# One 2 MB gradient store cut into a 120-row and an 8-row transfer, eight pairs before the end of a decoder-block backward pass

## The chip, the cores and the metric

The kernel runs on one core of a Trainium2 chip. The metric is device time in microseconds (us) for one launch, the median of several executions. The launch computes the forward pass and all gradients of one decode step of a transformer block. It uses the core's five engines: TensorE (PE in the profile, its weight loads PEld), VectorE (DVE), ScalarE (ACT), GpSimd (POOL) and SyncE (SP). Data moves between HBM and the on-chip memory through the core's 16 DMA engines. Nearly all transfers here are issued by SP, in the order in which the program writes them.

## The reference

The block takes a token for each of 4 sequences (512 values each), 32 heads of 128, and a key and a value cache of 4096 positions for each of the 4 x 32 = 128 heads:

```
q      = layernorm(x) @ wq                           # 4 x 32 heads x 128
p      = softmax(q . k_cache / sqrt(128))            # 128 heads x 4096
o      = p . v_cache
h      = x + o @ wo
out    = h + (silu(LN(h) @ w1) * (LN(h) @ w3)) @ w2
grads  = vjp(out; grad_out) for x, k_cache, v_cache, wq, wo, w1, w3, w2
```

The two large results are the gradients of the caches. For each head, dV is the outer product of p (4096) and the gradient of o (128), and dK is the outer product of dS (4096) and q (128). Each is 4096 x 128 values in bf16, 1 MB a head, so 128 MB for dK and 128 MB for dV. The caches, which must be read, are of the same size.

## The kernel before, in words

All large tiles live in one tile `arena` of 23 slots, each a little over 8 KB on each of 128 partitions (`Slot`); `Slot2` takes two neighbouring slots, for two heads at once. A slot is taken when a tile is made and given back when its last reader has been issued; the framework puts in the semaphore waits that make the reuse safe, so a slot whose content is being stored is written again only when that store has landed.

**First part** (to about 700 us). For each head, K and V are loaded (1 MB each, lines 181 and 189), scores and softmax are computed, and K and V are reduced to what the later steps need.

**Second part.** V is loaded again, transposed in place on TensorE and ScalarE (lines 805 and 806), multiplied with the gradient of o to give dP (line 1363 for pairs), and turned into dS. VectorE then writes the outer products. The first 32 heads (`SP = 32`) are done one at a time; the other 96 are done as 48 pairs (`NT`), t = 0 to 47. A pair's gradient takes two slots and is stored by one transfer of 128 rows of 8192 bf16 values, 16 KB a row: 64 rows for each of the two heads. The function that does it is `grad_pair` (line 1441). Its VectorE work is `outer_pair` (line 1434), one multiply of 128 x 8192, and its store is line 1444. It is called for dV (`out_3`) by `more_V` and for dK (`out_2`) by the loop over t. The loop, for each t: loads the V of pair t + 3 where one is left (line 1331), runs that pair's transposes and dP with a slice of the side work between them (`side`: the gradients of the weights), runs `more_V`, which keeps dV a little ahead of dK, and then stores dK of pair t:

```
grad_pair(out_2, t, pdS[t // 2][:, t % 2], reps["rq", "p", t // B][:, t % B, :])
```

SP issues all of this in one queue. After the dK store of t = 40, that queue holds 16 more transfers: a load of V (2 MB), two pair stores, the last load of V, the last 1 MB store of the side work (line 1190), and eleven pair stores.

The row view that the store uses is

```
ap[b, h:h + 2].rearrange("h (p j) d -> (h p) (j d)", p=P // 2)
```

which is 128 rows of 16 KB, one for each partition. Completion of SP's transfers is counted on eight semaphores in turn: each transfer takes the next one and is issued only when the transfer that used it eight issues before has landed.

Of the kernel before, what the change touches and what calls it, by code (L numbers as in the profile page):

```python
# [28 lines left out]
def kernel(  # L29
# [22 lines left out]
    nc = tc.nc  # L52
    P = nc.NUM_PARTITIONS
# [5 lines left out]
    Dh = A_k_cache.shape[3]  # L59
# [6 lines left out]
    SJ = Sk // P  # L66
# [144 lines left out]
    for i in range(2):  # L211
        t = fcon.tile([P, 64], BF16, name=f"onesw{i}")
# [4 lines left out]
    def ones_window(col):  # L217
# [11 lines left out]
                          in_=rowg[:, None, :, None].to_broadcast([P, 4, 8, 4]))  # L229
# [758 lines left out]
    with ExitStack() as c2:  # L988
# [325 lines left out]
        NT = (NH - SP) // 2  # L1314
# [8 lines left out]
        def two_heads(ap, t):  # L1323
            b, h = t % B, H0 + t // B * 2
            return ap[b, h:h + 2].rearrange("h (p j) d -> (h p) (j d)", p=P // 2)
# [107 lines left out]
        def outer_pair(dst, col2, row):  # L1433
            nc.vector.tensor_tensor(  # L1434
                out=dst.rearrange("p (j r t) -> p j r t", r=Dh // 2, t=2),
                in0=col2[:, :, None, :].to_broadcast([P, 2 * SJ, Dh // 2, 2]),
                in1=row.rearrange("p (r t) -> p r t", t=2)[:, None, :, :].to_broadcast([P, 2 * SJ, Dh // 2, 2]),
                op=ALU.mult,
            )

        def grad_pair(out_ap, t, col2, row):
            g_ = Slot2()
            outer_pair(g_.t[:, 0:2 * SJ * Dh], col2, row)
            nc.sync.dma_start(out=two_heads(out_ap, t), in_=g_.t[:, 0:2 * SJ * Dh])
            g_.give()

        O0, S0, S1, L, LP = 2, 21, 35, 5, 3
# [2 lines left out]
        def more_V(upto):  # L1450
            while gvd["n"] < min(SP, upto):
                s = gvd["n"]
                P_pairs(s)
                replicate("rdo", s - s % REP)
                grad_V(s)
                P_pairs(s + 1)
                P_pairs(s + 2)
                gvd["n"] += 1
                if s % REP == 2 and s + 2 < SP:
                    replicate("rdo", s + 2)  # L1460
                elif s % REP == 2:
                    replicate_pair("rdo", 0)
                if s >= SP - 2:
                    P2_pair(s - SP + 2)
            while gvd["t"] < NT and SP + 2 * gvd["t"] + 2 <= upto:
                t = gvd["t"]
                P2_pair(t)
                replicate_pair("rdo", t // B)
                grad_pair(out_3, t, pP2.pop(t), reps["rdo", "p", t // B][:, t % B, :])
                P2_pair(t + 1)  # L1470
                gvd["t"] += 1
                if t % B == 2:
                    replicate_pair("rdo", t // B + 1)
# [59 lines left out]
        for t in range(NT):  # L1533
            s = SP + 2 * t
            load_pairs(t + LP)
            if t % B == 2:
                replicate_pair("rq", t // B + 1)
            if t + LP < NT:
                front_pair(t + LP, lambda: side(s))
            else:  # L1540
                if t + LP == NT:
                    rows_out()
                    rows_T()
                side(s)
            more_V(s + 2 + lead_V(s))
            grad_pair(out_2, t, pdS[t // 2][:, t % 2], reps["rq", "p", t // B][:, t % B, :])
            if t % 2 == 1 and t + 1 < NT:
                group_dS_pair((t + 1) // 2)
            side(s + 1)
# [31 lines left out]
```

## Time and profile before

| what | value |
|---|---|
| median of 3 runs | 1683.99 us (1683.85 to 1684.81) |
| the profiled execution, its own time | 1683.33 us |
| its span, first to last instruction | 1681.5 us |
| mean granted TensorE clock | 0.869 |
| busy share of PE, DVE, ACT, POOL | 74%, 74%, 57%, 25% |
| moved by DMA | 707.16 MB, mean 421 GB/s |
| pair stores of 2048 KB (line 1444) | 96, median 27.5 us from issue to landing |
| loads of V for a pair, 2048 KB (line 1331) | 48, median 31.7 us |
| one `outer_pair` on DVE | 4.4 us |

The page gives engine shares for the whole span, a row of 40 slices with the mean busy share of the 16 DMA engines, and the chain of work that ended last. For one stage, the table of stretches is the view to read: a line has the start and end of the stretch, its length, the busy time of each engine with its number of instructions, the granted clock, the mean busy share of the 16 DMA engines and the rate in GB/s. A share of 0.06 is one engine of the sixteen at work. In the order of instructions, "SPq" is SP issuing a transfer; the time beside it covers all that is merged into the line, waits included.

### The profile page before, as it was taken

Reading aid. Unit: us, or ns where it says so; the run is one execution under the profiler, and the core shown is the slowest. Engines: PE = TensorE matmul, PEld = TensorE weight load, DVE = VectorE, ACT = ScalarE, POOL = GpSimd, SP = SyncE. Lnnn points to the kernel's source line nnn. Section 1 sums busy time; section 2 is a strip of 40 time slices with the busy share of each in tenths; the row PEclk is TensorE's granted clock in tenths of the full one; section 3 lists DMA queues with packets and bytes.
Section 4 is the critical chain, followed back from the end, with each engine's and each line's share of the span. In section 5 each row is a group of like instructions: output and inputs, shape, how many; then the busy total and the mean of one; then the engine's idle time right before and its main releaser. Section 6 shows DMA issues by size and latency. Waiting matters only on the chain.

```text
span 1681.5 us, 33231 instructions
## 1 busy us (share of the span) xinstructions
PE 1243.9 (74%) x13784; PEld 874.1 (52%) x13784; DVE 1238.8 (74%) x1204; ACT 957.5 (57%) x1482; POOL 412.9 (25%) x732
## 2 busy tenths in 40 slices
PE   5889888888888888877777657567766776776750
PEld 4777776667666776644433335444444443444430
DVE  5989899999999987767766467576655656655682
ACT  3455454445445544677666556666665676676650
POOL 1221222222232223444552323211100011111110
PEclk9999999999999999999999878886667667676675
DMA  9999999999999999999999999999999999999996
GB/s 401 424 425 425 425 424 425 424 425 424 418 424 412 424 404 407 412 409 425 426 426 428 430 430 429 429 430 430 430 430 429 431 429 431 430 429 429 431 431 277
DMA packets 80983, 707.16 MB, mean 421 GB/s; under 512 B 8748, under 2 KB 12984, under 8 KB 15296
## 3 DMA queue, kind: packets, MB, share of 16 engines
q1 hardware_dynamic: 80416, 704.94, 99.4%
q8 instruction: 108, 1.77, 0.4%
q14 instruction: 43, 0.35, 0.0%
q0 software_dynamic: 416, 0.10, 0.0%
HBM read 422.59 MB, written 282.34 MB: 419 GB/s over the span
## 4 chain that ended last, share of the span: by engine, by line
DMA 40%; DVE 8%; PE 5%; ACT 4%; issue 3%; POOL 2%; DVEq 0%; SPq 0%; ACTq 0%; POOLq 0%
DMA out_dram<-arena 37%; DVE arena L1434 6%; ACT arena L806 3%; DMA arena<-in_A_v_cache_dram 3%; POOL zd L1246 1%; PE pt_tps L805 1%; PE M_ps L475 1%; DVE arena L460 1%; PE dq_ps L1032 1%; PE dP_ps L1280 1%; DMA arena<-arena 0%; PE pt_wo L613 0%; POOL P L1251 0%; ACT Pn L439 0%; POOL arena L1431 0%
## 5 line engine op out<-in xcount | busy, mean ns | idle before, releaser
L806 ACT COPY arena<-pt_tps 128x1024 bf16<-128x1024 bf16 x512 | 491.1, 1026 | 239.2 <-PE pt_tps L805 236.1
L805 PE MATMUL pt_tps<-ident_f,arena 128*128 128x128 f32 x2048 | 397.0, 346 | 195.4 <-DMA arena<-in_A_v_cache_dram 111.7
L805 PEld LDWEIGHTS pt_tps<-ident_f,arena 128*128 128x128 f32 x2048 | 290.8, 175 | 362.7 <-issue 187.3
L1434 DVE TENSOR_TENSOR arena<-arena 128x8192 bf16<-128x8192 bf16 x48 | 212.4, 4425 | 206.6 <-DMA out_dram<-arena 176.3
L475 PE MATMUL M_ps<-arena 128*128 128x130 bf16 x4096 | 285.9, 222 | 43.7 <-DMA arena<-in_A_v_cache_dram 43.2
L460 DVE TENSOR_TENSOR arena<-arena 128x4096 bf16<-128x4096 bf16 x128 | 292.4, 2285 | 24.3 <-POOL arena L456 24.3
L475 PEld LDWEIGHTS <-arena 128*128 128x128 bf16 x4096 | 252.3, 99 | 65.1 <-DMA arena<-in_A_v_cache_dram 58.1
L1434 DVE TENSOR_TENSOR arena<-dS,arena 128x8192 bf16<-128x8192 bf16 x48 | 212.4, 4426 | 63.6 <-DMA out_dram<-arena 63.6
L367 DVE STREAM_TRANSPOSE arena<-arena 128x512 f32<-128x512 f32 (+1 forms) x321 | 250.5, 796 | 0.0
L362 ACT COPY arena<-pt_tps 128x1024 bf16<-128x1024 bf16 x128 | 129.4, 1012 | 189.4 <-PE pt_tps L361 147.4
L373 POOL TENSOR_TENSOR W<-qrep,wmask 128x128 bf16<-128x128 bf16 x128 | 120.0, 938 | 85.6 <-PE S_ps L393 71.2
L1431 POOL COPY arena<-arena 128x128 bf16<-128x128 bf16 x48 | 45.2, 941 | 374.5 <-DVE arena L1434 248.6
L456 POOL COPY arena<-P_all 128x64 bf16<-128x64 bf16 x128 | 32.4, 253 | 413.1 <-ACT P_all L450 410.0
L1343 POOL COPY arena<-arena 64x4 bf16<-64x4 bf16 x96 | 78.5, 818 | 127.7 <-PE dP_ps L1363 118.2
L1363 PE MATMUL dP_ps<-arena 128*32 128x512 bf16 x768 | 85.3, 478 | 8.4 <-ACT arena L806 7.9
L450 ACT COPY P_all<-pt_P 32x64 bf16<-32x64 bf16 x256 | 51.9, 203 | 54.6 <-PE pt_P L446 52.4
L820 DVE TENSOR_TENSOR arena<-dS,arena 128x4096 bf16<-128x4096 bf16 x32 | 73.3, 2292 | 12.7 <-DMA out_dram<-arena 12.3
L361 PE MATMUL pt_tps<-ident_b,arena 128*128 128x128 bf16 x1024 | 80.5, 223 | 0.0
L820 DVE TENSOR_TENSOR arena<-P,arena 128x4096 bf16<-128x4096 bf16 x29 | 66.4, 2293 | 18.4 <-DMA out_dram<-arena 17.3
L485 PE MATMUL kP_ps<-arena,onesw 128*32 128x512 bf16 x1024 | 79.6, 388 | 0.0
L393 PE MATMUL S_ps<-arena,W 128*32 128x256 bf16 x1536 | 75.2, 286 | 0.5 <-DVE arena L367 0.2
L439 ACT ACTIVATE Pn<-E,rl 128x1024 bf16<-128x1024 f32 x64 | 73.7, 1151 | 3.2 <-DVE rl L436 3.2
(257 smaller groups left out, 1402.3 us busy)
## 6 DMA issues: line engine op xcount, KB each, us to landing
out_dram<-arena SPq DMA_DIRECT2D x96, 2048.0 KB, 27.5
arena<-in_A_v_cache_dram SPq DMA_DIRECT2D x160, 1024.0 KB, 15.9
arena<-in_A_k_cache_dram SPq DMA_DIRECT2D x128, 1024.0 KB, 15.5
arena<-in_A_v_cache_dram SPq DMA_DIRECT2D x48, 2048.0 KB, 31.7
out_dram<-arena SPq DMA_DIRECT2D x72, 1024.0 KB, 19.8
arena<-in_A_wq_dram SPq DMA_DIRECT2D x8, 1024.0 KB, 17.8
arena<-in_B_w_dram SPq DMA_DIRECT2D x8, 896.0 KB, 14.9
out_dram<-arena SPq DMA_DIRECT2D x6, 896.0 KB, 26.5
```

The source lines that it names most:

```text
L361: nc.tensor.transpose(pt[:, i, :], Kn[:, c * GW + i, :], ident_b[:])
L362: nc.scalar.copy(out=KT[:, c * GW:(c + 1) * GW, :], in_=pt[:])
L367: nc.vector.transpose(out=KT[:, c * w_:(c + n) * w_], in_=Kn[:, c * w_:(c + n) * w_])
L373: nc.gpsimd.tensor_tensor(out=W[:, hl], in0=qrep[:, :, s:s + 1].to_broadcast([P, 4, 32]), in1=wmask[:, hl, None, :].to_broadcast([P, 4, 32 ...
L460: nc.vector.tensor_tensor(out=PK[:, :, 0:Dh].rearrange("p j (r t) -> p j r t", t=2), in0=Ks[s].heads().rearrange("p j (r t) -> p j r t", t=2),
L475: nc.tensor.matmul(hold["M"][:], lhsT=Vn[:, j, :], rhs=PK[:, j, :], start=(j == 0), stop=(j == SJ - 1))
L485: nc.tensor.matmul(hold["kP"][32 * q:32 * (q + 1), :, :], lhsT=ones_window(w), rhs=PK[:, j0:j0 + 4, 0:Dh], start=(w == 0 and c == 0), stop ...
L805: nc.tensor.transpose(ptw[:, jj, :], w[:, 4 * g + jj, :], ident_f[:])
L806: nc.scalar.copy(out=v.rearrange("p (j d) -> p j d", d=Dh)[:, g * GW:(g + 1) * GW, :], in_=pt[:])
L820: nc.vector.tensor_tensor(out=dst.rearrange("p j (r t) -> p j r t", t=2), in0=col2[:, :, None, :].to_broadcast([P, SJ, Dh // 2, 2]), in1=r ...
L1363: nc.tensor.matmul(rows["acc"][32 * c:32 * (c + 1), :], lhsT=zt[t % B][:, k, ZP - m:ZP - m + 32], rhs=words_of(v, 2 * c + u, k), start=(pl ...
L1434: nc.vector.tensor_tensor(out=dst.rearrange("p (j r t) -> p j r t", r=Dh // 2, t=2), in0=col2[:, :, None, :].to_broadcast([P, 2 * SJ, Dh / ...
```

## The change

Inside `grad_pair`, one store out of 96 is cut in two: the dK store of the pair t = NT - 8 = 40. Partitions 0 to 119 go in a first transfer and partitions 120 to 127 in a second one right behind it. Together they carry the same 2 MB to the same addresses. All other stores are issued as one transfer as before. The slots are given back after the last of the transfers.

```diff
         def grad_pair(out_ap, t, col2, row):
             g_ = Slot2()
             outer_pair(g_.t[:, 0:2 * SJ * Dh], col2, row)
-            nc.sync.dma_start(out=two_heads(out_ap, t), in_=g_.t[:, 0:2 * SJ * Dh])
+            cuts = (0, 120, P) if out_ap is out_2 and t == NT - 8 else (0, P)
+            for p0, p1 in zip(cuts, cuts[1:]):
+                nc.sync.dma_start(out=two_heads(out_ap, t)[p0:p1], in_=g_.t[p0:p1, 0:2 * SJ * Dh])
             g_.give()
```

In the order of instructions, SP has one row more (527 instead of 526); the order on the other engines is the same. The semaphore that each later transfer takes moves on by one, and the waits with it. The next tile in the slots of the cut store waits for two semaphores instead of one.

## The prediction

> **What bounds the kernel now.** I read the page's slices first, then the stretches at the end, then the DMA view of a stretch, SP's and DVE's order around the cut store, and the chain of waits. The page:
>
> ```profile
> span 1681.5 us, 33231 instructions
> PE 1243.9 (74%) x13784; PEld 874.1 (52%) x13784; DVE 1238.8 (74%) x1204; ACT 957.5 (57%) x1482; POOL 412.9 (25%) x732
> DMA  9999999999999999999999999999999999999996
> GB/s 401 424 425 425 425 424 425 424 425 424 418 424 412 424 404 407 412 409 425 426 426 428 430 430 429 429 430 430 430 430 429 431 429 431 430 429 429 431 431 277
> ```
>
> No compute engine is above 74%, and the DMA engines are busy in every slice but the last, at 429 to 431 GB/s late in the run. So the second half is bound by the transfers. The last slice has only 277 GB/s, and it decides what a late store costs. Stretches at the end (start:end, length, busy of each engine, clock, DMA share, GB/s):
>
> ```profile
> 1640.00:1650.00 10.00, 0.00 (x0) 0.00 (x0) 10.00 (x3) 0.00 (x0) 0.00 (x0) 0.50 1.00 429
> 1650.00:1660.00 10.00, 0.00 (x0) 0.00 (x0) 2.03 (x1) 0.00 (x0) 0.00 (x0) 0.50 1.00 428
> 1660.00:1664.00 4.00, 0.00 (x0) 0.00 (x0) 0.00 (x0) 0.00 (x0) 0.00 (x0) 0.50 0.89 381
> 1664.00:1668.00 4.00, 0.00 (x0) 0.00 (x0) 0.00 (x0) 0.00 (x0) 0.00 (x0) 0.50 0.58 250
> 1668.00:1669.00 1.00, 0.00 (x0) 0.00 (x0) 0.00 (x0) 0.00 (x0) 0.00 (x0) 0.50 0.12 49
> 1669.00:1670.00 1.00, 0.00 (x0) 0.00 (x0) 0.00 (x0) 0.00 (x0) 0.00 (x0) 0.50 0.08 33
> 1670.00:1679.40 9.40, 0.00 (x0) 0.00 (x0) 0.00 (x0) 0.00 (x0) 0.00 (x0) 0.50 0.06 26
> 1679.40:1681.50 2.10, 0.00 (x0) 0.00 (x0) 0.00 (x0) 0.00 (x0) 0.00 (x0) 0.50 0.00 0
> ```
>
> DVE is done at 1652, and the rest is drain. Until 1660 all 16 DMA engines work (1.00). From 1664 to 1668 some nine do (0.58 x 16 = 9.3). From about 1669 to 1679.4 the share is 0.06, which is one engine of 16, at 26 GB/s. So one engine finishes some 10 us after all others, and the time of the kernel is the time of that engine. It has moved no more gradient bytes than the others: every transfer SP issues has 128 rows, or a multiple, over 16 engines. It is just later. I also followed the packet records of the trace back from the end, each packet beginning as the engine's last one ends. That gives 16 unbroken rows of packets. The late engine trails the next latest by 0.7 us at 881 us, 3.3 at 1083, 6.2 at 1316, 9.1 at 1566 and 10.3 at the end. Its 16 KB packets of pair stores take 621 ns each from start to start, those of three others 608 to 611; on loads of V it is no slower (609). So it is one and the same engine, steadily slower on stores, and not a late accident. None of the 16 rows shows an idle gap above 0.1 us after 1353 us.
>
> The DMA view from 1600 to 1660 us, packets and small packets:
>
> ```profile
> DMA packets 1844, 25.80 MB, mean 430 GB/s; under 512 B 205, under 2 KB 205, under 8 KB 205
> q1 hardware_dynamic: 1842, 25.77, 100.5%
> ```
>
> There is one small packet to 8 data packets ((1842 - 205) / 205 = 7.98). That is one engine's part of one transfer: 128 rows over 16 engines are 8 rows each, closed by one small completion packet.
>
> SP's order around the cut store, and the DVE work that waits for its slots:
>
> ```profile
> 1570.28 0.33 SPq L1190 DMA_DIRECT2D out_dram<-arena  x1
> 1576.37 0.33 SPq L1444 DMA_DIRECT2D out_dram<-arena  x1
> 1576.92 0.34 SPq L1331 DMA_DIRECT2D arena<-in_A_v_cache_dram  x1
> 1580.71 10.78 SPq L1444 DMA_DIRECT2D out_dram<-arena  x2
> 1591.69 0.34 SPq L1331 DMA_DIRECT2D arena<-in_A_v_cache_dram  x1
> 1603.19 0.33 SPq L1190 DMA_DIRECT2D out_dram<-arena  x1
> ...
> 1604.03 4.42 DVE L1434 TENSOR_TENSOR arena<-dS,arena 128x8192 bf16<-128x8192 bf16 x1 [6.90 <-DMA out_dram<-arena]
> ```
>
> The store at 1576.37 is the one that is cut (the transfers left behind it are those of t = 40). At 1604.03, after 6.90 us of waiting, DVE writes into its slots again: 27.7 us from issue to landing, of which some 5 are its own packets. The rest is queue.
>
> **The change part by part.** *What each engine has to move.* Before, each of the 16 engines has 8 packets of the store. After, the first part has 120 rows = 15 x 8, the second 8 rows. No row of this trace shows a transfer of 120 or of 8 rows. The nearest is that of 128: eight rows to an engine, in all its transfers. By it fifteen engines keep 8 packets of the first part and the one with the last eight rows gets none; the second part's 8 packets are bounded by one each on eight engines (+1 on these) and all eight on one (+8 on that one). I take one each, as rows were spread over as many engines as there were.
>
> [...]
>
> *Price of eight packets.* At 428 GB/s over 16 engines one engine moves 26.75 GB/s, so 8 x 16,384 B = 131,072 B take 4.90 us. From 26 GB/s of the lone engine it is 5.04, from the packet records 8 x 607 ns = 4.86 in the drain and 8 x 621 ns = 4.97 before it. I take 4.9, ends 4.8 and 5.1. One packet more costs 0.6 us.
>
> *Which engine is relieved.* If the late engine is the one with the last eight rows, it has 4.9 us less to move behind 1576 us and is never idle after, so the end moves by the whole 4.9. The next latest engines end at about 1669.2, or 1669.8 with one packet more, still 4.7 us ahead of the relieved one at 1674.5. Nothing takes the place of the gain. If it is another engine, the end moves by 0 or +0.6 us. The trace doesn't number the engines; by rows alone it may be any. I take the last. This is the step that carries the forecast, and it is a bet on position and not a reading: a single slow engine that is slow only when it reads the arena's rows is likelier tied to an end of the row range than to its middle.
>
> [...]
>
> *SP.* One issue more, 0.33 us at 1576.7, and the load of V behind it goes out that much later. The semaphores move on by one, so the store at 1580.71 now also waits for the load issued at 1549.66; with 31.7 us, the median of such loads, that one lands at 1581.4: 0.7 us later. Behind these wait the next store, the next load and DVE only through slots. The cost is nothing, because the late engine's queue at that time is some 22 us deep (27.6 us from issue to landing less 5) and the others' 12. If that cover were gone it would be 1.0 us at most.
>
> *DVE.* The slots come free when both parts have landed. Without the late engine that is earlier by up to the lag there (9 us), so the 6.90 us wait at 1604.03 shrinks, by as much as all of it. With it among the fifteen it stays, or grows by 0.6. Either way it is off the path: what DVE writes at 1604 is issued at 1608.4 and moved by the late engine only from about 1631 on.
>
> *Sum.* -4.9 (8 packets) + 0 (SP) + 0 (DVE) = -4.9 us. The profiled execution took 1683.33 us, its span 1681.5; after, 1678.4 and 1676.6. The median of the runs, 1683.99, lies 0.66 above the profiled one, so I forecast 1679.1 (-0.29%).
>
> **The rivals.**
>
> *Same: the late engine is not the one left out.* For it: nothing in the trace numbers the engine. Against it: only the bet on position. Time: 1684.0 if it gets the usual 8 packets, 1684.6 if it gets one of the second part's. [...]
>
> *Slower: 120 rows are not a multiple of 16, and the first part is moved by few engines.* Place: the store at 1576.37. With eight engines at 15 rows each, and one row more from the second part, eight engines have +8 packets: the late one, if among them, ends 4.9 us later, 1688.9. With a single engine for all 120 it has +112, 68 us: an engine that ended at 1662 would end at 1730, so some 1734 for the kernel (the median lies 4.5 above the last packet). It decides from 6 packets more on the late engine (3.4 / 0.607), or from 23 more on one of those that end at 1669 (10.3 + 3.4 = 13.7 us). For it: no transfer in this trace has such a count of rows. Against it: the other transfers, of 128, 256 and 1024 rows, all spread evenly over 16.
>
> **How the numbers follow.** Late engine left out: 0.66. Same: 0.22. Slower: 0.12. I give 0.2% (3.4 us) as what a measurement of this kernel can tell from no change; the three runs spread over 0.96 us. The cases fall into these classes one by one: faster 0.66, same 0.22, slower 0.12. The likeliest has 1678.0 to 1680.2 as its own range (4.8 to 5.1 off, with the runs' spread of about 1 us). The same case reaches 1684.6 and, with the spread, 1685.2. The range 1678.0 to 1685.2 leaves out the slower case alone.
>
> **What the profile after would show.** Right: the stretch with a share of 0.06 is some 5 us long instead of 10, the last packets end near 1674.6 and the span is about 1676.6, while the fall from 1.00 to 0.58 stays between 1660 and 1668; the first part of the store lands sooner than 27.7 us after issue, and DVE's 6.90 us wait shrinks. Same: the lone stretch keeps its 10 us and the wait its 6.9. Slower: a longer stretch at 0.06, or at 0.5 with eight engines. The prediction would be wrong if the late engine has another number, if it is another engine from run to run, or if 120 rows are dealt out in another way.

## The result, and the profile after

The median went from 1684.45 us to 1689.48 us: a ratio of 1.0031, 95% interval 1.0021 to 1.0041, five microseconds slower. The profiled execution of the changed kernel took 1689.24 us with a span of 1687.5 us, 6.0 more than before. It went the other way than forecast, by almost exactly the forecast's size.

The page of the changed kernel: span, DMA slices, rates and packets.

```profile
span 1687.5 us, 33232 instructions
DMA  9999999999999999999999999999999999999995
GB/s 401 424 425 425 425 425 425 425 425 424 420 424 405 424 415 402 405 411 427 425 426 430 430 429 430 430 429 430 430 431 429 430 429 431 429 429 432 402 424 253
DMA packets 80990, 707.16 MB, mean 419 GB/s; under 512 B 8755, under 2 KB 12991, under 8 KB 15303
```

The packet line of the page before:

```profile
DMA packets 80983, 707.16 MB, mean 421 GB/s; under 512 B 8748, under 2 KB 12984, under 8 KB 15296
```

The same bytes are moved. The third slice from the end stands out: 402 GB/s, where before it had 431, and its DMA digit is still 9. Small packets (under 512 B) are 8755; before, 8748. Sixteen completions of the one store went and 23 came: 15 + 8. So the rows were dealt out as the prediction read them, 120 over 15 engines and 8 over eight, with the 16 KB data packets unchanged in number.

Now the stretch in which the cut store is moved, first before, then after (start:end, length, busy of each engine, clock, DMA share, GB/s):

```profile
1584.00:1588.00 4.00, 2.78 (x14) 2.24 (x14) 1.29 (x1) 3.96 (x6) 0.00 (x0) 0.80 1.01 432
1588.00:1592.00 4.00, 3.47 (x20) 2.39 (x20) 3.94 (x4) 3.15 (x5) 0.00 (x0) 0.62 1.01 432
1592.00:1596.00 4.00, 3.41 (x20) 0.85 (x16) 3.95 (x4) 2.33 (x5) 0.00 (x0) 0.50 0.99 426
1596.00:1600.00 4.00, 3.75 (x15) 2.42 (x14) 1.13 (x1) 2.75 (x4) 0.29 (x1) 0.50 1.02 434
```

```profile
1584.00:1588.00 4.00, 3.05 (x13) 2.62 (x14) 1.19 (x1) 3.54 (x6) 0.00 (x0) 0.68 0.99 408
1588.00:1592.00 4.00, 2.95 (x16) 2.21 (x16) 3.94 (x4) 3.15 (x5) 0.00 (x0) 0.74 1.04 354
1592.00:1596.00 4.00, 3.20 (x24) 1.01 (x23) 3.95 (x4) 2.96 (x5) 0.00 (x0) 0.83 0.95 315
1596.00:1600.00 4.00, 0.40 (x3) 0.10 (x2) 1.25 (x1) 0.72 (x2) 0.29 (x1) 0.60 1.02 373
```

This is the reading that matters. The share stays at 0.95 to 1.04 while the rate falls from 430 to 315 GB/s. The engines did not run dry; their packets took longer. The packet records, which list the start, length and size of every packet, say how much longer: mostly from 1585 to 1605 us, 16 KB packets of about 1.2 us (up to 2.4) appear beside those of 0.61 us, on most of the 16 engines, and a few 8 KB packets take up to 1.18 instead of 0.31 us. Summed over the 16 engines, what packets took beyond 0.61 or 0.31 us is 42 engine-microseconds from 1576 to 1615 (below, "slowed packets" is this sum).

The drain at the end of the changed kernel:

```profile
1668.00:1670.00 2.00, 0.00 (x0) 0.00 (x0) 0.00 (x0) 0.00 (x0) 0.00 (x0) 0.50 0.50 213
1670.00:1672.00 2.00, 0.00 (x0) 0.00 (x0) 0.00 (x0) 0.00 (x0) 0.00 (x0) 0.50 0.34 147
1672.00:1674.00 2.00, 0.00 (x0) 0.00 (x0) 0.00 (x0) 0.00 (x0) 0.00 (x0) 0.50 0.29 123
1674.00:1676.00 2.00, 0.00 (x0) 0.00 (x0) 0.00 (x0) 0.00 (x0) 0.00 (x0) 0.50 0.12 49
1676.00:1680.00 4.00, 0.00 (x0) 0.00 (x0) 0.00 (x0) 0.00 (x0) 0.00 (x0) 0.50 0.06 25
1680.00:1685.00 5.00, 0.00 (x0) 0.00 (x0) 0.00 (x0) 0.00 (x0) 0.00 (x0) 0.50 0.07 29
```

One engine is still alone for some 10 us. Its last packet has moved back by 6.0 us (1679.5 to 1685.5) and that of the next latest engine by 6.7 (1669.2 to 1675.8), while the first engines to finish moved by less than 3. In DVE's order the wait for the cut store's slots, 6.90 us before, has become 12.82:

```profile
1610.07 4.43 DVE L1434 TENSOR_TENSOR arena<-dS,arena 128x8192 bf16<-128x8192 bf16 x1 [12.82 <-DMA out_dram<-arena]
```

### The profile page after: what moved, and what is told of

It is laid out like the page before. It is cut to its first block, busy times and chain, and to the rows that moved or that the text cites. A ratio compares the mean times of both kernels' runs of the same rounds, so it can differ in the third digit from the quotient of the medians.

```text
span 1687.5 us, 33232 instructions
## 1 busy us (share of the span) xinstructions
PE 1248.9 (74%) x13784; PEld 878.7 (52%) x13784; DVE 1238.7 (73%) x1204; ACT 957.9 (57%) x1482; POOL 420.6 (25%) x732
## 2 busy tenths in 40 slices
DMA packets 80990, 707.16 MB, mean 419 GB/s; under 512 B 8755, under 2 KB 12991, under 8 KB 15303
## 4 chain that ended last, share of the span: by engine, by line
DMA 45%; DVE 9%; PE 3%; issue 2%; POOL 2%; ACT 1%; DVEq 0%; SPq 0%; ACTq 0%; POOLq 0%
DMA out_dram<-arena 41%; DVE arena L1434 7%; DMA arena<-in_A_v_cache_dram 3%; DVE arena L820 1%; DMA arena<-arena 1%; POOL zd L1246 1%; PE M_ps L475 1%; DVE arena L460 1%; ACT arena L806 0%; PE pt_w L604 0%; POOL P L1251 0%; ACT Pn L439 0%; POOL arena L1431 0%; DVEq L1578 0%; PE kP_ps L485 0%
## 5 line engine op out<-in xcount | busy, mean ns | idle before, releaser
L1343 POOL COPY arena<-arena 64x4 bf16<-64x4 bf16 x96 | 88.6, 923 | 123.7 <-PE dP_ps L1363 114.2
L425 ACT ACTIVATE E<-S_ps,nm 128x256 f32<-128x256 f32 x64 | 30.4, 475 | 88.3 <-DVE nm L422 88.3
L1007 PE MATMUL gps<-arena 4*128 4x512 bf16 x110 | 46.6, 453 | 39.7 <-ACT arena L1001 39.7
```

The costliest lines, as they stand in the source:

```text
L1343: nc.gpsimd.tensor_copy(out=zt[t % B][r_, :, ZP + 2 * i:ZP + 2 * i + 2], in_=zt[B][r_, :, s - SP:s2 - SP + 1:B])
```

## The experiments

Three theories stood after this, all of them guesses. P: packets slow one another when engines read certain rows at the same time, as if several rows shared a port of limited rate; with a store of 128 rows they don't meet, with one of 120 or of 8 they do. L: the late engine was dealt more packets. Q: two transfers in that place, or the waits that move by one semaphore, delay what follows.

**Two halves by columns.** The same place, two transfers, but all 128 rows in each.

```diff
-            cuts = (0, 120, P) if out_ap is out_2 and t == NT - 8 else (0, P)
+            cuts = (0, SJ * Dh, 2 * SJ * Dh) if out_ap is out_2 and t == NT - 8 else (0, 2 * SJ * Dh)
-            for p0, p1 in zip(cuts, cuts[1:]):
+            for c0, c1 in zip(cuts, cuts[1:]):
-                nc.sync.dma_start(out=two_heads(out_ap, t)[p0:p1], in_=g_.t[p0:p1, 0:2 * SJ * Dh])
+                nc.sync.dma_start(out=two_heads(out_ap, t)[:, c0:c1], in_=g_.t[:, c0:c1])
```

> The same store (dK of t = 40) is cut by columns instead of rows: two transfers of 128 rows x 8 KB. Rows stay with the engines that carry them in all other stores, but there are two transfers, one more issue on SP and the same shift of the semaphores. Theory P (ports: with 120 rows the engines read rows that other engines' packets are reading at the same time, and such packets take 1.2 us instead of 0.61): no slower than before, within 0.1% (1 us). Theory L (load: the late engine was dealt up to 8 packets more): no slower either. Theory Q (two transfers in that place, or the shifted waits, delay what follows): about +5 us, as with the 120 and 8 rows.

Measured: 1684.76 us against 1685.05 for the kernel before, ratio 0.9998 (0.9989 to 1.0008). The stretch of this kernel and the DVE wait:

```profile
1588.00:1592.00 4.00, 2.22 (x12) 1.06 (x10) 3.78 (x1) 3.05 (x5) 0.00 (x0) 0.93 1.02 434
1592.00:1596.00 4.00, 3.99 (x26) 2.17 (x26) 3.89 (x7) 2.80 (x3) 0.00 (x0) 0.57 1.05 446
1596.00:1600.00 4.00, 2.54 (x16) 1.37 (x15) 2.65 (x1) 3.42 (x6) 0.29 (x1) 1.00 0.98 418
...
1605.68 4.43 DVE L1434 TENSOR_TENSOR arena<-dS,arena 128x8192 bf16<-128x8192 bf16 x1 [7.02 <-DMA out_dram<-arena]
```

The rate stays at 418 to 446 GB/s, the wait at 7.0, and slowed packets sum to 1.4 engine-us. Two transfers, the extra issue and the shifted waits cost nothing that shows. Q falls.

**112 and 16 rows.**

```diff
-            cuts = (0, 120, P) if out_ap is out_2 and t == NT - 8 else (0, P)
+            cuts = (0, 112, P) if out_ap is out_2 and t == NT - 8 else (0, P)
```

> The same store cut at row 112: 112 rows = 16 x 7 and 16 rows = 16 x 1, so each of the 16 engines keeps 8 packets in all if rows are dealt evenly. Theory P: slower than before, by 2 to 8 us, because seven rows an engine do not begin where the eight rows of the other stores begin; packets of 1.2 us in the stretch where the store is moved. Theory L: no change, within 1 us. Theory Q: about +5 us, as with the 120 and 8 rows.

Measured: 1690.7 us, ratio 1.0034 (1.0022 to 1.0046). The packet records show 7 + 1 packets on the engines, the late one too, so each kept its eight, and yet the price is that of 120 and 8. Slowed packets sum to 33 engine-us. L falls as the cause: every engine has the number of packets that it had before, and the loss is there all the same. What differs from a whole store is that an engine's rows come as seven and one instead of eight.

**The 120 rows alone.**

```diff
-            cuts = (0, 120, P) if out_ap is out_2 and t == NT - 8 else (0, P)
+            cuts = (0, 120) if out_ap is out_2 and t == NT - 8 else (0, P)
```

> The first part alone: rows 120 to 127 of that store are left out, so eight rows of dK stay unwritten and 0.13 MB less is moved. Theory P, if the 120 rows are the misfit: still +2 to +5 us against before, with 1.2 us packets; if only the eight rows are (eight engines reading one group of rows), no slower than before. Theory L: the fifteen engines have 8 packets, as before, so 0, or -4.9 us if the late engine is the one left out. Theory Q: 0, as there is one transfer again.

Measured: 1689.3 us, ratio 1.0024 (1.0015 to 1.0034), 27 engine-us of slowed packets. So the larger part alone is a misfit and carries most of the loss. What the eight rows add is blurred in the medians (1.0031 against 1.0024, with overlapping intervals), but the late engine's own packets show it. Followed through the same transfers in each profile, from the one that begins at 1576 us in the kernel before to the last packet, the late engine takes 5.9 us longer than before with 120 and 8 rows, 5.9 with 112 and 16, 4.4 with the 120 rows alone and 0.1 with the column halves. The eight rows add 1.5 us here: the one packet more (0.6) and slowed packets (0.9).

**Streams of nothing but stores.** A kernel without computation, from one tile:

```
phase(rows(0, 128))                                  # 8 stores each, then a DVE memset of the tile
phase(rows(0, 120, 128))
phase(rows(0, 120))
phase(rows(120, 128), 16)
phase(rows(0, 112, 128))
phase(rows(0, 64, 128))
phase([(0, P, 0, N // 2), (0, P, N // 2, N)])
phase(rows(0, 35, 70, 105))
phase(rows(0, 16), 16)
phase(rows(0, 128))
```

> No computation: ten phases of stores from one tile, each phase begun when the one before has landed: 8 stores of 128 rows; of 120 + 8; of 120 alone; 16 of the last 8 rows; 8 of 112 + 16; of 64 + 64; of two column halves; of 35 + 35 + 35 rows; 16 of rows 0 to 15; 8 of 128 rows again. Theory P: 128 rows and column halves at about 430 GB/s (39 us for 16.8 MB); 120 + 8, 120 alone and 112 + 16 clearly below (under 350 GB/s); the last 8 rows, and rows 0 to 15, far below what 8 and 16 engines can do (216 and 430 GB/s), as all read a few ports. [...] Theory L: 120 + 8 at the pace of an engine with 9 packets of 0.61 us, 5.5 us a store or 382 GB/s; 112 + 16 and 64 + 64 at 430; the last 8 rows at 216 and rows 0 to 15 at 430 GB/s, less what the fixed cost of each takes.

The memset that ends each phase waits for all its stores. In DVE's order of this kernel the bracket holds that wait, which is the length of the phase:

```profile
1.65 3.47 DVE L46 MEMSET a<- 128x4096 uint32 x1 [1.65 <-PEq L90]
46.89 3.47 DVE L61 MEMSET a<- 128x4096 uint32 x1 [41.76 <-issue]
123.26 3.47 DVE L61 MEMSET a<- 128x4096 uint32 x1 [72.91 <-issue]
180.74 3.47 DVE L61 MEMSET a<- 128x4096 uint32 x1 [54.00 <-issue]
227.35 3.47 DVE L61 MEMSET a<- 128x4096 uint32 x1 [43.13 <-issue]
295.89 3.47 DVE L61 MEMSET a<- 128x4096 uint32 x1 [65.08 <-issue]
353.61 3.47 DVE L61 MEMSET a<- 128x4096 uint32 x1 [54.25 <-issue]
399.54 3.47 DVE L61 MEMSET a<- 128x4096 uint32 x1 [42.45 <-issue]
486.72 3.47 DVE L61 MEMSET a<- 128x4096 uint32 x1 [83.71 <-issue]
533.50 3.47 DVE L61 MEMSET a<- 128x4096 uint32 x1 [43.31 <-issue]
578.71 3.47 DVE L61 MEMSET a<- 128x4096 uint32 x1 [41.73 <-issue]
```

The same phases as stretches, in the same order (busy of DVE and POOL, clock, DMA share, GB/s):

```profile
6.00:46.00 40.00, 0.00 (x0) 0.00 (x0) 1.00 0.99 419
50.40:122.00 71.60, 0.00 (x0) 0.00 (x0) 1.00 0.73 234
126.70:180.00 53.30, 0.04 (x1) 0.00 (x0) 1.00 0.83 295
184.20:227.00 42.80, 0.01 (x1) 0.00 (x0) 1.00 0.47 49
230.80:295.00 64.20, 0.02 (x1) 0.00 (x0) 1.00 0.85 261
299.40:353.00 53.60, 0.00 (x0) 0.00 (x0) 1.00 0.91 313
357.00:399.00 42.00, 0.09 (x1) 0.00 (x0) 1.00 0.96 399
403.00:486.00 83.00, 0.01 (x1) 0.00 (x0) 1.00 0.42 166
490.20:533.00 42.80, 0.00 (x0) 0.00 (x0) 1.00 0.95 98
537.00:578.00 41.00, 0.00 (x0) 0.00 (x0) 1.00 0.97 409
```

Read them against the first. Eight stores of 128 rows take 41.8 us, at 419 GB/s in their stretch. Cut by columns, 42.5. Cut at row 120, 72.9: a store goes from 5.2 to 9.1 us, so one cut costs (72.9 - 41.8) / 8 = 3.9 us on average. Of this the 120 rows alone take 54.0, and the eight rows the other 18.9, 2.4 us a cut. 112 + 16 takes 65.1 and 64 + 64 takes 54.3 (313 GB/s), and three pieces of 35 rows, on seven engines (share 0.42), take 83.7 for fewer bytes, so any cut by rows that was tried costs.

These are means over eight stores, and the cost is not spread evenly. In the packet records the mean 16 KB packet of the 120-row phase takes 1.12 us in the first eighth of its packets and 0.61 from the sixth eighth on; with 64 + 64 it is 1.20 and again 0.61. That fits engines that begin in step and drift apart, which is a reading and not shown. With 120 + 8 it falls from 1.13 only to some 0.71.

The two smallest forms show the slowing at its strongest. Rows 0 to 15 use all 16 engines (share 0.95) and move 98 GB/s; the last eight rows use eight engines (0.47) and move 49. In the packet records their 16 KB packets, one row to an engine, take 2.53 us each, about four times 0.61, as if four engines shared what one engine gets in a whole store, some 27 GB/s (16 KB in 0.61 us). Call what they share a port: 49 GB/s is then nearly two of them and 98 nearly four, an estimate from these rates.

The first packets of the other phases point the same way. In the packet records of the 120-row phase 14 of the 15 first packets take 0.95 to 1.28 us and one takes 0.64. With 64 + 64 all 16 first packets take 1.13 to 1.28, and in whole stores, which run at 419 GB/s, every first packet takes 0.61 to 0.64. A packet of some 1.2 us is twice 0.61, as if two engines met on one port, and one of the 15 had none to meet. That is a reading: the records list no rows, so which rows share a port, how many ports there are and how the rows of a store are dealt is not shown. P stands in this form: packets slow one another, up to four times, and whether they do depends on the rows of the transfer. Row and address in HBM go together in all these stores, so a conflict on the HBM side was not run apart. Against such a conflict: in the kernel the late engine's slowed packets include some of a load of V (1.2 us in all), which reads other addresses.

**Eight cuts.**

```diff
-            cuts = (0, 120, P) if out_ap is out_2 and t == NT - 8 else (0, P)
+            cuts = (0, 120, P) if out_ap is out_2 and NT - 16 <= t < NT - 8 else (0, P)
```

> The cut into 120 and 8 rows is made in the eight dK stores t = 32 to 39 instead of t = 40 alone. Theory P (ports): each cut costs again; by the streams of stores alone, (72.9 - 41.8) / 8 = 3.9 us for one cut, so +31 us, and +40 us by the 5 us of the one cut; DMA share stays near 1.0 with the rate well below 430 GB/s in that stretch. A rival, that the one cut only costs a disturbance that the next ones share (engines thrown out of step once): +5 to +10 us in all. Theory L (one engine has more packets): 8 times one packet of 0.6 us on the late engine, +5 us.

Measured: 1718.29 us against 1685.15, ratio 1.0196 (1.0168 to 1.0225), which is +33 us or 4.1 a cut (3.5 to 4.7). The same stretches, first before, then of this kernel:

```profile
1450.00:1500.00 50.00, 33.05 (x191) 19.44 (x189) 30.77 (x12) 33.45 (x44) 12.21 (x10) 0.77 1.01 431
1500.00:1550.00 50.00, 34.95 (x170) 21.24 (x171) 29.72 (x17) 31.25 (x40) 6.49 (x11) 0.67 1.01 430
1550.00:1600.00 50.00, 36.78 (x180) 22.85 (x178) 29.48 (x16) 33.27 (x42) 7.39 (x7) 0.64 1.01 430
```

```profile
1450.00:1500.00 50.00, 33.81 (x167) 20.69 (x166) 25.27 (x11) 30.24 (x40) 7.64 (x8) 0.66 1.00 392
1500.00:1550.00 50.00, 28.82 (x151) 16.84 (x150) 26.09 (x11) 26.72 (x35) 5.70 (x9) 0.68 0.99 366
1550.00:1600.00 50.00, 32.20 (x153) 21.05 (x154) 24.27 (x16) 28.58 (x35) 4.77 (x7) 0.60 0.99 363
```

The cuts cost again and again, and the share stays at 0.99 to 1.00. It is not one disturbance that later cuts share. That the mean is close to the 3.9 us of the bare stream is no proof of a fixed price, as that mean holds a costly start and a cheaper end.

**The last store on seven engines.** All other stores whole.

```diff
-            cuts = (0, 120, P) if out_ap is out_2 and t == NT - 8 else (0, P)
+            cuts = (0, 35, 70, 105, 126, P) if out_ap is out_2 and t == NT - 1 else (0, P)
```

> All stores whole again, but the last one (dK of t = 47) is cut into rows 0-34, 35-69, 70-104, 105-125 and 126-127. By the count of completions after the 120 and 8 rows (15 + 8), a cut's rows go to as many engines as divide them, at most 16: here 7, 7, 7, 7 and 2, so nine engines and, if it is not among the seven, the late one have nothing of the last store. If the late engine is among the nine and packets were never slowed: its last packet 4.9 us earlier, at 1674.6, and the seven engines with 18 or 19 packets end at about 1675; kernel -4 us. Theory P with the late engine among the nine: the pieces read the late engine's ports while it is still on the stores before, 105 rows took 10.5 us in the stream of 35-row pieces, so the seven end at about 1677 to 1680 and the gain is -3 to +1 us. If the late engine is one of the seven: it has 10 packets more, +6 us or more.

Measured: 1693.5 us, ratio 1.0052 (1.0035 to 1.0068), slower than the change itself. The last 11 us of its DMA view:

```profile
DMA packets 21, 0.28 MB, mean 25 GB/s; under 512 B 4, under 2 KB 4, under 8 KB 4
```

One engine is alone again (25 GB/s), with 17 data packets and 4 completions. In the packet records these are groups of 5, 5, 5 and 3, its shares of the pieces of 35, 35, 35 and 21 rows (the first of the 18 packets began just before the stretch), and nothing of the piece of two. So the late engine is one of the seven. Ten packets more than its usual eight are 6.1 us. Its last packet ends 9.7 us later than before (1689.2 against 1679.5); the other 3.6 I put down to slowed packets in the crowded drain, but didn't measure apart. No cut by rows tried here beats the kernel before.

## Why the prediction was wrong, point by point

*What bounds the kernel* held: the last engine's row of packets sets the end, with a share of 0.06 to 0.07 from 1676 to 1685 us in the profile after and of 0.07 from 1676 to 1688 with the last store on seven engines. In the profile after, this row has gaps of only 0.04 us in all behind 1566 us, so the 6 us lie in its packets and not in a wait for work.

*What each engine has to move* held: 15 + 8 completions, and on the late engine 8 packets of the first part and one of the second.

*The bet on position* failed. In the packet records of the changed kernel the late engine has all its 8 packets of the first part and one of the second, so it was not the one left out; and in the last experiment it is among the seven. Even with unchanged packets it would have been +0.6 us and not -4.9. The text called this step a bet, and then gave it 0.66 of the chance; sixteen engines that the trace doesn't number support no such figure.

*Price of eight packets* is the step that failed and made the sign: the lost bet takes away the 4.9 us gained, and this step brings in the 5 us lost. The sum took each packet at 0.6 us whoever moves it and whatever rows it reads. That figure was measured on transfers of whole 128 rows alone. In transfers of other rows packets took up to 2.5 us in the bare stream and 1.2 and more in the kernel. For the late engine the slowed packets sum to 5.6 us, and the one packet more to 0.6: 6.2, where the two profiled executions differ by 6.0. It lost most of it not in the cut store (0.9 us), but in the two transfers of 16 KB packets before it, a pair store (3.3) and a load of V (1.2), at a time when the engines ahead of it were already in the cut store. By theory P they read rows that shared a port with its own, which the records don't list.

*SP and DVE* at no cost held. The column halves have the same extra issue and the same shifted semaphores and cost nothing. The store that was to go out 0.7 us later went out 1.1 later (1581.85 instead of 1580.71).

*The rivals.* The slower one had the right place and nearly the right time (1688.9 for eight engines, 1689.48 measured), but the wrong mechanism: it counted eight packets more on the late engine, and the runs show one more, worth 0.6 us. That its time came out is luck. What the runs show in its place, packets of 1.2 us and more instead of 0.61 on most of the 16 engines, was missing from the list altogether, and the range ended at 1685.2. *Same* had the late engine's packets right in its second time, eight and one more (1684.6), but priced them at 0.6 us each as the forecast did. Measured here, a cut costs 3.9 us in the stream, as a mean, and 5.0 in the kernel.

## What to carry to other kernels

With a DMA share near 1.0 at some 430 GB/s, as here, a transfer's rows are part of its price: eight whole stores take 41.8 us alone, cut by columns 42.5, cut once by rows 54.3 to 72.9. Cut a full 128-row store, of 16 KB rows as here, by columns if it must be cut, not by rows. Price a new shape by a bare stream of that shape, not by packets of another, and look at the first store of the stream apart from the last. And read share and rate together: in this kernel a share at 1.0 with a falling rate (430 to 315 GB/s) meant slowed packets, not missing work.

## What was not expected of the hardware

Packets slow one another by as much as four times: one of 16 KB takes 0.61 us in a whole store and 2.53 us when eight engines move the rows 120 to 127, or sixteen the rows 0 to 15, one row each. Two halves of 64 rows run at 313 GB/s, where a whole store runs at 419: their packets begin at 1.20 us and are back at 0.61 before the phase ends, which fits engines that drift apart until they no longer meet, again a reading and not shown. And the engine that trails by 10 us in the whole kernel doesn't trail without computation: in the first phase of the stream all 16 engines end within 0.24 us of each other (45.29 to 45.53 us). Its lateness on stores, 621 against 608 ns a packet, thus needs something of the whole kernel that the stream leaves out; what that is was not tried.
